# Three more two-level down products, deep weights stored in order of use, and later tokens' norms from row sums

## The chip, the cores and the metric

The kernel runs on one core of a Trainium2 chip. The time is device microseconds of one launch, from its first to its last instruction and a little around them. The kernel before was run four times: a median of 1454.92 us, from 1453.96 to 1455.33. One of these runs was profiled: 1455.33 us.

## What is computed

Four layers act in turn on x, 2048 tokens of 1024 features: A, B, A, B, each adding to x. A is linear attention with 32 heads, B is a gated MLP with an inner width of 3584:

```python
def _B_ref(x, W_gate, W_up, W_down):
    gate = jnp.einsum("bsd,df->bsf", x, W_gate)
    up = jnp.einsum("bsd,df->bsf", x, W_up)
    gate = gate * (lambda x, dt: x.astype(dt))(gate > 0, gate.dtype)
    h = gate * up
    return jnp.einsum("bsf,fd->bsd", h, W_down)

x = A_x
x = x + _A_ref(_layernorm(x, axis=-1), A_wqkv, A_wo)
x = x + _B_ref(_layernorm(x, axis=-1), B_W_gate, B_W_up, B_W_down)
x = x + _A_ref(_layernorm(x, axis=-1), A_wqkv, A_wo)
x = x + _B_ref(_layernorm(x, axis=-1), B_W_gate, B_W_up, B_W_down)
```

The layer norm has no weights: mean and variance over the 1024 features, 1e-5 under the root. Both B layers use the same three matrices, and so do both A layers.

## The kernel before

The tokens are 16 tiles of 128, and x stays in SBUF in float32 all the time. Layers are numbered 0 to 3, so B is layers 1 and 3. A B layer is worked in two chunks c of 8 tiles, written (1,0), (1,1), (3,0) and (3,1). A chunk is first 14 GLU units u, each for 256 of the 3584 columns (`glu`, L1129, with its matmuls on L1144), and then a down stage.

All large products use the Strassen–Winograd scheme: two operands cut in 2 x 2 blocks, seven products of blocks instead of eight, and sums of blocks before and after. In a down stage (`down_deep`, L1212) the left operand is h and its sums (four blocks of 512 tokens by 1792 features, "e" for two of the sums), the right one is W_down in blocks of 1792 by 512: the raw blocks 11, 21 and 22, and the sums T1 to T4, which are made once, on VectorE (`load_d`, `sums_d`, L1062 and L1076), and kept in DRAM in `td`. A plain product (`product`, L1247) is 4 token tiles by 14 matmuls of 512 columns. Results are added from PSUM into x by `onto` (L1263). A product of this stage can be *deep* (`deep`, L1291): the scheme once more inside it, with seven sub-products of two halves of 7 matmuls of 256 columns. Its left sums S1 to S4 are made on VectorE (`inner`, L1285, adds on L1283). Within a deep product three PSUM banks x, y and z are in use; ScalarE copies the first and fifth sub-products (L1315), VectorE makes the z sum out of the sixth and the copied fifth (L1325), and `put` adds each quarter of the result into x. T1's result goes into both token halves, so that its put (`put_both`, L1350) is two adds. The right sums of a deep product, four blocks of 896 by 256, are made once on VectorE (`load_dd`, `sums_dd`, L1011 and L1030) and stored in DRAM in `dd`.

Which products are deep is in `is_deep` (L974): T1, 22 and T4, in all chunks but (1,0), where an older function `down` (L1386, matmuls on L1418) does all seven plain. The deep blocks are made while the GLU of (1,1) runs, units 1 to 9. `td` is made earlier, the last two of its seven pairs of rows during the GLU of (1,0), one sum a unit in units 4 to 11. That GLU also makes the sums of the gate and up weights for later chunks (`make_gu`, L1050 to L1058, once per unit, ScalarE's queue stores them as tg and tu).

Weights come through a ring of slots in SBUF, filled ahead of use in the order in which they are used (`plan_B`, L955, on SP's DMA queue; plain entries on L968). A deep product takes four ring entries (`load_deep`, L993): an entry holds two blocks (the last one), a raw one read out of the matrix or `td` in rows of 256 elements (`load_raw`, L1003) and a made one out of `dd` (L1007). SP's queue works in order, and also holds the transposes of normed tiles (L399), the moves of x tiles to DRAM and back (`send_away`, `bring_back`, L258), and the stores of `td` and `dd` (L1078 and in `sums_dd`).

The normed tiles for a B layer are made in two ways. For tiles 0 to 7 the attention's last addition into x also sums each row (a scalar_tensor_tensor with an accumulator, L768, into `acc`), and ScalarE makes the sum of squares with an accumulating Square (`ln_norm_sums`, L204, L214 to L220). The later tiles 8 to 15 take statistics on VectorE (BN statistics, L162 to L167, then a shift on L196), in the down stage of (1,0) or (3,0) for the chunk that follows. The A layer that follows takes its first eight tiles' statistics in the same way. A normed tile is transposed by SP's DMA (L399), and then VectorE makes its sums for the GLU's scheme (`sums_x`, L1108, L1118 to L1121).

The program's order is written by hand: work for engines beside TensorE is put into a list `later` with a delay in ticks, a tick being called after each group of matmuls, so the delays set where in VectorE's and SP's in-order queues something lies. `behind` and `issue_after` hold an instruction back until after a given one in its queue. Where nothing holds it, an instruction may stand in its queue ahead of the place where it was written, as soon as its inputs are there: so the statistics for layer 2's first tiles, written in the down stage of (1,1), lie in that of (1,0).

Of the kernel before, what the change touches and what calls it, by code (L numbers as in the profile page):

```python
# [92 lines left out]
class _Net:  # L93
    def __init__(self, tc, ctx, x_d, wqkv_d, wo_d, wg_d, wu_d, wd_d, out_d):
# [34 lines left out]
        self.td = self.spill.tile([P, self.U, 4, NW], F16, name="td")  # L129
        self.tw = {n: self.spill.tile([P, 8, NW], F16, name=f"t{n}") for n in ("q0", "q1", "k0", "k1")}  # L130
        self.dd = {p: self.spill.tile([P, 4, self.U // 2, NW // 2], F16, name=f"dd{p}") for p in self.DEEP}
# [15 lines left out]
        self.x = [self.xall[:, t, :] for t in range(self.ST)]  # L147

        self.xb = [x[:, D // 2:D].bitcast(BF16) for x in self.x]
        self.xnT, self.xn, self.pk, self.slabs, self.xs, self.acc = {}, {}, {}, {}, {}, {}  # L150
# [29 lines left out]
    def ln_norm(self, layer, t):  # L180

        nc = self.nc
        if layer % 2 and t < self.NS:
            return self.ln_norm_sums(layer, t)
# [19 lines left out]
    def ln_norm_sums(self, layer, t):  # L204

        nc, src, acc = self.nc, self.x[t], self.acc[layer]
# [206 lines left out]
    def ln_later(self, layer, q, first, step, lag):  # L413
        for j in range(QT):
            self.ln_at(first + j * step, layer, q * QT + j, lag)
# [37 lines left out]
    def layer_A(self, l, last_ln):  # L453
# [298 lines left out]

        def out_unit(sc, j, n2):
            t = sc * QT + j
            ps = self.ps.tile([P, NW], F32, tag="a")
            for g in range(G):
                nc.tensor.matmul(ps, lhsT=pqT[sc][:, g, j * P:(j + 1) * P],  # L757
                                 rhs=T[g // 4][:, g % 4, n2 * NW:(n2 + 1) * NW],
                                 start=(g == 0), stop=(g == G - 1))
            cols = slice(n2 * NW, (n2 + 1) * NW)  # L760
            xs = self.x[t][:, cols]


            x0 = self.xb[t][:, cols] if l == 0 else xs
            if t < self.NS:
                if last_ln not in self.acc:
                    self.acc[last_ln] = self.const.tile([P, 2 * self.NS], F32, name=f"acc{last_ln}")
                self.last_x = nc.vector.scalar_tensor_tensor(  # L768
                    out=xs, in0=ps, scalar=0.0, in1=x0, op0=ALU.add, op1=ALU.add,
                    accum_out=self.acc[last_ln][:, 2 * t + n2:2 * t + n2 + 1])  # L770
            else:
                self.last_x = nc.vector.tensor_tensor(out=xs, in0=x0, in1=ps, op=ALU.add)


        def out_pairs(sc):
# [38 lines left out]
            def products():  # L814
# [4 lines left out]
                def onto(i, n, bank):  # L819
                    xs = half(self.x[sc * QT + i], n)  # L820
                    nc.vector.tensor_tensor(out=xs, in0=xs, in1=bank, op=ALU.add)

                for m, bank, start, n in ((1, X, True, None), (5, V, True, (2, 1)), (6, Y, False, (0, 1)),
                                          (2, X, False, (0, 0)), (7, Y, False, (2, 1)),
                                          (3, V, False, (0, 1)), (4, Y, False, (2, 0))):
                    for i in range(2):
# [6 lines left out]
                        else:  # L833
                            onto(n[0] + i, n[1], bank[i])
# [137 lines left out]
    DEEP = ("T1", "22", "T4")  # L972

    def is_deep(self, l, c, p):  # L974
        return (l, c) != (1, 0) and p in self.DEEP

    def order_d(self, l, c):
        if (l, c) == (1, 0):
            return "11", "21", "T1", "T2", "T3", "22", "T4"
        return "11", "21", "T1", "T2", "22", "T3", "T4"  # L980

    def src_d(self, p, us, cols=slice(0, NW)):
        if p[0] == "T":
            return self.td[:, us, self.T_AT[p], cols]
        n = (int(p[1]) - 1) * NW
        return self.wd_v[:, int(p[0]) - 1, us, n + cols.start:n + cols.stop]
# [6 lines left out]
    def load_deep(self, t, p, e):  # L993

        half, hn = self.U // 2, NW // 2
        v = self.deep_view(t)
        lo, hi = slice(0, half), slice(half, 2 * half)
        made = {0: (1, 0), 1: (0, 1), 2: (0, 2), 3: (0, 3)}[e]
        raw = {0: (0, lo, 0), 1: (1, hi, 0), 2: (1, hi, hn)}.get(e)

        def load_raw():
            src = self.src_d(p, raw[1], slice(raw[2], raw[2] + hn))
            self.nc.sync.dma_start(out=v[:, raw[0], :, :].bitcast(src.dtype), in_=src)  # L1003

        if raw and raw[0] == 0:
            load_raw()
        self.nc.sync.dma_start(out=v[:, made[0], :, :].bitcast(F16), in_=self.dd[p][:, made[1], :, :])  # L1007
        if raw and raw[0] == 1:
            load_raw()

    def load_dd(self, p):  # L1011

        half = self.U // 2
        self.deep_t = t = [self.slot(f"dd{p}{i}", [P, half, NW]) for i in range(2)]
        for out, us in ((t[0][:, :, :], slice(0, half)),
# [3 lines left out]
            self.nc.sync.dma_start(out=out.bitcast(src.dtype), in_=src)  # L1019

    def sums_dd(self, p, n):

        t = self.deep_t
        hn = NW // 2
        (b11, b12), (b21, b22) = ([x[:, :, i * hn:(i + 1) * hn] for i in range(2)] for x in t)
        f16 = lambda a: a.bitcast(F16)
        raw = f16 if p[0] == "T" else lambda a: a
        out, a, b = ((f16(b11), raw(b12), raw(b11)), (f16(b12), raw(b22), raw(b12)),
                     (f16(b22), raw(b22), f16(b11)), (f16(b21), raw(b21), f16(b22)))[n]
        self.nc.vector.tensor_tensor(out=out, in0=a, in1=b, op=ALU.subtract)  # L1030
        if n == 1:
            self.later.at(2, lambda: [self.nc.sync.dma_start(out=self.dd[p][:, m, :, :], in_=f16(b))
                                      for m, b in ((0, b11), (2, b12))])
        if n == 3:
            self.later.at(2, lambda: [self.nc.sync.dma_start(out=self.dd[p][:, m, :, :], in_=f16(b))
                                      for m, b in ((3, b21), (1, b22))])
# [31 lines left out]
    def sums_d(self, t, u, ops=range(4)):  # L1068

        T = t[:, :, :, :].bitcast(F16)  # L1070
        for n in ops:
# [5 lines left out]
            if n == 3:  # L1077
                self.later.at(2, lambda: self.nc.sync.dma_start(  # L1078
                    out=self.td[:, u:u + 2, :, :], in_=T))
# [43 lines left out]
    def ln_chunk(self, l, c, first, step, lag, after):  # L1123
        for j in range(QT):
            for h in range(2):
                self.ln_at(first + (2 * j + h) * step, l, (2 * c + h) * QT + j, lag, after)
            self.later.at(first + (2 * j + 1) * step + lag + (5 if l == 3 else 3), lambda j=j: self.sums_x(l, c, j))
# [84 lines left out]
    def down_deep(self, l, c, hT, final):  # L1212
# [27 lines left out]
        free = of_h(0)  # L1240
        S1, S2, S4, S3 = (cut(free[k], j) for k in range(2) for j in range(2))
# [43 lines left out]
        def inner(A):  # L1285
            (a11, a21), (a12, a22) = ([cut(A[k], j) for j in range(2)] for k in range(2))
            return (a11, a12, a21, a22), list(sums(((S1, a21, a22, ALU.add), (S2, S1, a11, ALU.subtract),
                                                    (S3, a11, a21, ALU.subtract),
                                                    (S4, a12, S2, ALU.subtract))))

        def deep(p, parts, put):  # L1291

            a11, a12, a21, a22 = parts
            B = {}

            def entry(e):
# [4 lines left out]
                lo, hi = lambda x: lambda i: x[:, i, :], lambda x: lambda i: x[:, (i + 1) % NK, :]  # L1301
                B.update(({1: lo(raw[:, 0]), 5: lo(made[:, 1])}, {6: lo(made[:, 0]), 2: hi(raw[:, 1])},
                          {7: lo(made[:, 0]), 3: hi(raw[:, 1])}, {4: lo(made[:, 0])})[e])

            def mm(m, A, bank, start=False):
                for j in range(2):
                    for i in range(NK):
                        nc.tensor.matmul(bank[:, j * H:(j + 1) * H],  # L1308
                                         lhsT=A[i // 2][:, i % 2, j * P:(j + 1) * P], rhs=B[m](i),
# [19 lines left out]
            put(1, 1, m5, False)  # L1329
# [3 lines left out]
            put(1, 1, y, True)  # L1333
            later.tick()
            mm(3, S4, z)
            put(0, 1, z, True)
            later.tick()
# [9 lines left out]

        both = self.xall[:, first:first + 2 * QT, :].rearrange("p (a j i) n -> p a j i n", a=2, i=2)
# [14 lines left out]

        product("11", raw(0), X, True, seed)
        parts, jobs = inner(of_e(e1))
        spread(jobs, 1, 3)
        product("21", raw(1), X, False, to(first, 0, X, True))
        for p, (_, b, _, _) in pairs:
            later.at(2 + p // 2, lambda b=b, p=p: v.tensor_tensor(out=b, in0=b, in1=part(e2, p),
                                                                 op=ALU.subtract))  # L1370
        deep("T1", parts, put_both)
        parts, jobs = inner(of_h(1))
        spread(jobs, 1, 2)
        product("T2", own(e2), Y, False, to(first, 1, Y, False))
        deep("22", parts, put_into(first, 1))
        parts, jobs = inner(of_h(3))
        spread(jobs, 1, 2)

        def third_done(j):
            to(second, 1, Y, True)(j)  # L1380
            to(second, 0, Y, False)(j)

        product("T3", raw(2), Y, False, third_done)
        deep("T4", parts, put_into(second, 0))

    def down(self, l, c, hT, final):  # L1386
        if (l, c) != (1, 0):
            return self.down_deep(l, c, hT, final)

        nc, later, ring, v = self.nc, self.later, self.ring, self.nc.vector  # L1390
        N = NW
        pairs = [(p, [x[:, b::4, :] for b in range(4)]) for p, x in enumerate(hT)]
        e1, e2 = ([self.slot(f"e{i}_{l}_{c}_{k}", dtype=F16) for k in range(2)] for i in (1, 2))
        part = lambda e, p: e[p // 4][:, (p % 4) * 2:(p % 4) * 2 + 2, :]
        with self.tc.issue_after(self.last_put.ins):
            for p, (a, _, g, d) in pairs:
                v.tensor_tensor(out=part(e1, p), in0=g, in1=d, op=ALU.add)
                v.tensor_tensor(out=part(e2, p), in0=part(e1, p), in1=a, op=ALU.subtract)
            for p, (a, _, g, d) in pairs:
                v.tensor_tensor(out=g, in0=a, in1=g, op=ALU.subtract)  # L1400
        raw = lambda b: lambda k: hT[k // 2][:, (k % 2) * 4 + b, :]
        own = lambda e: lambda k: e[k // 8][:, k % 8, :]
        X = [self.ps.tile([P, N], F32, tag="a", name=f"dx{j}") for j in range(QT)]
        Y = [self.ps3.tile([P, N], F32, tag="b", name=f"dy{j}") for j in range(2)]
        Y += [self.kvp.tile([P, N], F32, tag=f"kv{j}", name=f"dy{2 + j}") for j in range(2)]
        V = []
# [172 lines left out]
```

## Time and profile before

| what | value |
| --- | --- |
| median of four runs | 1454.92 us (1453.96 to 1455.33) |
| profiled execution | 1455.33 us, its span 1453.6 us |
| TensorE clock | 1.00 |
| TensorE busy | 1440.6 us, 99% of the span |
| VectorE busy | 952.4 us, 66% |
| ScalarE busy | 590.2 us, 41% |
| GLU of (1,0) | about 222 to 397 us, with the attention's last products of layer 0 among its first units |
| down stages | about 397 to 479 us (1,0), 651 to 740 (1,1), 1117 to 1200 (3,0), 1369 to the end (3,1) |

The profile gives, for each engine, the time in which it was busy. A window's row gives the busy time and number of instructions per engine in that stretch, the granted TensorE clock, and how busy the DMA engines were. The chain follows the work that ended last back to the start: each piece is an instruction (or several alike) that the next one waited for, or that stood before it on its engine. A group row gives instructions of one line and shape: their number, busy time, mean, and the idle time of the engine ahead of them with what ended it. A line number is that of the kernel before.

### The profile page before, as it was taken

The page shows a single profiled execution, that of the slowest core. Times are in us where ns is not written, and L with a number is a line of the kernel's source. Part 1 is how long each engine was busy: PE and PEld are TensorE (multiplying, and loading weights), DVE is VectorE, ACT ScalarE, POOL GpSimd, SP SyncE. Part 2 cuts the span into 40 slices and gives each one's busy share as a digit, 9 for nine tenths or more (in the row PEclk, how much of TensorE's full clock was granted, in tenths as well). Part 3 has the DMA queues.
Part 4 walks back from the last instruction along what each step waited for, and adds up shares of the span by engine and source line. Part 5 has one row for each costly group of instructions (what it writes and reads, how often), then busy time and mean ns, then how long its engine had stood idle before and what let it go on. Part 6 is the DMA issues. An engine that isn't in the chain of part 4 may idle for free.

```text
span 1453.6 us, 19816 instructions
## 1 busy us (share of the span) xinstructions
PE 1440.6 (99%) x7271; PEld 696.8 (48%) x7304; DVE 952.4 (66%) x1748; ACT 590.2 (41%) x1059; POOL 308.5 (21%) x221
## 2 busy tenths in 40 slices
PE   9999999999999999999999999999999999999998
PEld 4444444444444444445654444444444564444456
DVE  7978698666594555449688886766445864444574
ACT  7872574233340333332168626633333213333300
POOL 1453861011100011110031586410111011111001
PEclk9999999999999999999999999999999999999999
DMA  9840797664559999846983119975444799444473
GB/s 287 226 167 8 177 216 202 195 207 159 202 179 254 346 348 357 263 128 213 274 267 88 58 30 265 266 231 194 145 145 143 213 287 319 145 146 145 152 250 126
DMA packets 350801, 291.56 MB, mean 201 GB/s; under 512 B 107152, under 2 KB 317200, under 8 KB 348784
## 3 DMA queue, kind: packets, MB, share of 16 engines
q1 hardware_dynamic: 342656, 269.00, 63.0%
q10 hardware_dynamic: 6560, 17.24, 3.1%
q0 software_dynamic: 1488, 4.07, 0.8%
q8 instruction: 57, 0.93, 0.3%
q14 instruction: 40, 0.33, 0.1%
HBM read 221.32 MB, written 44.30 MB: 183 GB/s over the span
## 4 chain that ended last, share of the span: by engine, by line
PE 86%; DVE 7%; POOL 2%; DMA 1%; issue 1%; ACT 1%; SPq 1%; DVEq 0%; ACTq 0%; POOLq 0%
PE yg L1144 10%; PE yu L1144 10%; PE ps L479 10%; PE xu L1144 6%; PE xg L1144 6%; PE ps L757 4%; PE dy L1256 4%; PE zg L1144 3%; PE zu L1144 3%; PE dx L1256 3%; PE vu L1144 3%; PE vg L1144 3%; PE dy L1418 2%; PE mx L561 2%; PE dv L1418 2%; PE dx L1418 2%
## 5 line engine op out<-in xcount | busy, mean ns | idle before, releaser
L1144 PEld LDWEIGHTS <-w 128*128 128x128 f16 (+1 forms) x3136 | 306.6, 98 | 371.5 <-issue 2.2
L1197 POOL TENSOR_TENSOR h<-m5u,m5g 128x512 f16<-128x512 f32 x56 | 72.0, 1285 | 723.6 <-DVE m5u L1193 593.3
L479 PE MATMUL ps<-w,xnT 128*128 128x512 bf16 x768 | 170.0, 380 | 0.0
L1180 DVE TENSOR_TENSOR zg<-yg,m5g 128x512 f32<-128x512 f32 x56 | 39.1, 699 | 171.9 <-PE yg L1144 168.5
L479 PEld LDWEIGHTS <-xnT 128*128 128x128 bf16 x768 | 74.3, 98 | 89.8 <-issue 1.4
L1144 PE MATMUL yg<-s,w 128*128 128x512 f16 x448 | 115.0, 379 | 0.1
L1144 PE MATMUL xg<-xnT,w 128*128 128x512 f16 x448 | 115.0, 379 | 0.0
L1144 PE MATMUL yu<-s,w 128*128 128x512 f16 x448 | 115.0, 379 | 0.0
L1144 PE MATMUL xu<-xnT,w 128*128 128x512 f16 x448 | 115.0, 379 | 0.0
L1152 ACT ACTIVATE m5g<-m5g 128x512 f32<-128x512 f32 x56 | 35.2, 629 | 178.9 <-DVE m5g L1193 178.9
L422 ACT ACTIVATE e<-e,eps 128x512 f32<-128x512 f32 x128 | 91.0, 720 | 3.2
L709 POOL TENSOR_TENSOR kvc<-pq,kvc 128x1024 f32<-128x1024 bf16 x32 | 78.4, 2450 | 53.6 <-DVE den L714 33.3
L757 PE MATMUL ps<-T,pqT 128*128 128x512 bf16 x374 | 83.0, 380 | 0.5
L1308 PEld LDWEIGHTS <-h 128*128 128x128 f16 x756 | 74.0, 98 | 12.0 <-issue 2.0
L1256 PEld LDWEIGHTS <-h 128*128 128x128 f16 x504 | 49.4, 98 | 59.5 <-DMA w<-td 1.0
L1155 DVE TENSOR_TENSOR h<-yu,r 128x512 f16<-128x512 f32 x56 | 38.7, 691 | 55.1 <-PE yu L1144 55.1
L500 POOL TENSOR_TENSOR kvc<-kvc,slab 128x512 f32<-128x512 f32 x46 | 57.2, 1249 | 75.9 <-DVE slab L425 72.7
L1256 PE MATMUL dx<-w,h 128*128 128x512 bf16 x327 | 72.5, 379 | 0.5
L1161 ACT ACTIVATE m5g<-vg 128x512 f32<-128x512 f32 x56 | 33.4, 597 | 93.1 <-PE vg L1144 83.0
L1193 DVE TENSOR_TENSOR m5u<-yu,m5u 128x512 f32<-128x512 f32 x56 | 38.7, 691 | 49.5 <-PE yu L1144 49.4
L1152 ACT ACTIVATE r<-yg 128x512 f32<-128x512 f32 x56 | 33.4, 597 | 85.6 <-PE yg L1144 85.6
L421 ACT ACTIVATE e<-ps 128x512 f32<-128x512 f32 x92 | 54.2, 590 | 29.0 <-PE ps L479 29.0
(242 smaller groups left out, 2384.2 us busy)
## 6 DMA issues: line engine op xcount, KB each, us to landing
w<-in_B_W_gate_dram SPq DMA_DIRECT2D x56, 512.0 KB, 5.9
w<-in_B_W_up_dram SPq DMA_DIRECT2D x56, 512.0 KB, 5.6
w<-tg SPq DMA_DIRECT2D x42, 512.0 KB, 7.2
w<-tu SPq DMA_DIRECT2D x42, 512.0 KB, 6.7
w<-td SPq DMA_DIRECT2D x20, 896.0 KB, 5.0
w<-in_B_W_down_dram SPq DMA_DIRECT2D x18, 896.0 KB, 4.9
w<-ddT SPq DMA_DIRECT2D x24, 448.0 KB, 5.3
w<-in_A_wqkv_dram SPq DMA_DIRECT2D x8, 1024.0 KB, 7.3
```

Source lines behind the costliest of these rows:

```text
L421: nc.scalar.activation(out=e, in_=ps, func=ACT.Relu, scale=-1.0)
L422: nc.scalar.activation(out=e, in_=e, func=ACT.Exp, scale=-1.0, bias=self.eps6[:, 0:1])
L479: nc.tensor.matmul(by_row(ps), lhsT=self.xnT[l, l_q][:, kt, j * P:(j + 1) * P], rhs=w[:, kt, :].rearrange("p (b i d) -> p i b d", i=R, d=H ...
L500: nc.gpsimd.tensor_tensor(out=ksum[:, cols], in0=ksum[:, cols], in1=pk, op=ALU.add)
L709: nc.gpsimd.tensor_tensor(out=prod, in0=pq_of[sc, j], in1=zrow, op=ALU.mult)
L757: nc.tensor.matmul(ps, lhsT=pqT[sc][:, g, j * P:(j + 1) * P], rhs=T[g // 4][:, g % 4, n2 * NW:(n2 + 1) * NW], start=(g == 0), stop=(g == G ...
L1144: nc.tensor.matmul(ps, lhsT=W[w][m][:, k, :], rhs=A[m][:, k, :], start=start and k == 0, stop=k == 3, skip_group_check=True)
L1152: self.last_relu = nc.scalar.activation(out=out, in_=ps, func=ACT.Relu)
L1197: nc.gpsimd.tensor_tensor(out=h[:, 3, :], in0=V["u"], in1=V["g"], op=ALU.mult)
L1256: nc.tensor.matmul(banks[j], lhsT=A(k)[:, j * P:(j + 1) * P], rhs=w[:, i, :], start=start and k == 0, stop=k == self.U - 1, skip_group_che ...
L1308: nc.tensor.matmul(bank[:, j * H:(j + 1) * H], lhsT=A[i // 2][:, i % 2, j * P:(j + 1) * P], rhs=B[m](i), start=start and i == 0 and j == 0 ...
L1418: nc.tensor.matmul(banks[j], lhsT=A(k)[:, j * P:(j + 1) * P], rhs=w[:, i, :], start=start and k == 0, stop=k == self.U - 1, skip_group_che ...
```

## The change

Five things are changed together.

1. Three more down products are deep: T1 and 22 in (1,0), and 21 in (3,1). In (3,1) the order is now 11, T2, T1, T3, 21, 22, T4. The function `down_deep` becomes the only `down`, with a case for each list.
2. `dd` holds all seven right blocks of a deep product, raw ones too, in order of use, so a ring entry is one contiguous DMA. `td` is laid out product by product instead of row pair by row pair; a pair is stored in four DMAs instead of one, and each deep sum in one of its own.
3. Where the deep blocks are made: those of 22 and T1 in the GLU of (1,0), T4's in the GLU of (1,1), those of 21 in the GLU of (3,0). The last two row pairs of `td` are loaded at unit 3 of (1,0) and their eight sums made in units 4 to 6.
4. All tiles of a B layer's norm use row sums (`add_up`), the later tiles too. The statistics of layer 2's first tiles are held until after unit 6 of the GLU of (1,1).
5. In T1 the put of the fifth sub-product moves behind that of the third (`early`), and closes that quarter instead of opening it.

```diff
-    DEEP = ("T1", "22", "T4")
+    DEEP = ("T1", "22", "T4", "21")
     def is_deep(self, l, c, p):
-        return (l, c) != (1, 0) and p in self.DEEP
+        return p in {(1, 0): ("T1", "22"), (3, 1): self.DEEP}.get((l, c), self.DEEP[:3])
     def order_d(self, l, c):
-        if (l, c) == (1, 0):
-            return "11", "21", "T1", "T2", "T3", "22", "T4"
+        if (l, c) == (3, 1):
+            return "11", "T2", "T1", "T3", "21", "22", "T4"
         return "11", "21", "T1", "T2", "22", "T3", "T4"
...
     def load_deep(self, t, p, e):
+        n = min(2, 7 - 2 * e)
+        self.nc.sync.dma_start(out=self.deep_view(t)[:, 0:n, :, :].bitcast(F16),
+                               in_=self.dd[p][:, 2 * e:2 * e + n, :, :])
...
+    def make_dd(self, p, at):
+        self.later.at(at, lambda: self.load_dd(p))
+        for n in range(4):
+            self.later.at(at + 18 + 4 * n, lambda n=n: self.behind(self.last_put, lambda n: self.sums_dd(p, n), (n,)))
...
             if n == 3:
-                self.later.at(2, lambda: self.nc.sync.dma_start(
-                    out=self.td[:, u:u + 2, :, :], in_=T))
+                self.later.at(2, lambda: [self.nc.sync.dma_start(
+                    out=self.td[:, m, u:u + 2, :], in_=T[:, :, m, :]) for m in range(4)])
...
     def ln_norm(self, layer, t):
-        if layer % 2 and t < self.NS:
+        if layer % 2:
             return self.ln_norm_sums(layer, t)
...
+        def add_up(t, n2, xs, ps, x0):
+            return nc.vector.scalar_tensor_tensor(
+                out=xs, in0=ps, scalar=0.0, in1=x0, op0=ALU.add, op1=ALU.add,
+                accum_out=self.acc[:, 2 * t + n2:2 * t + n2 + 1])
...
             mm(2, a12, x)
             put(0, 0, x, True)
-            put(1, 1, m5, False)
+            early = p != "T1"
+            if early:
+                put(1, 1, m5, False)
             later.tick()
             entry(2)
             mm(7, S3, y)
-            put(1, 1, y, True)
+            put(1, 1, y, early)
             later.tick()
             mm(3, S4, z)
             put(0, 1, z, True)
+            if not early:
+                put(1, 1, m5, True)
...
-                    if u in (3, 7):
-                        d = self.U - 4 + u // 4 * 2
-                        wd[d] = self.load_d(d)
-                    if 3 < u < 12:
-                        self.later.at(4, lambda d=self.U - 4 + (u - 4) // 4 * 2, n=(u - 4) % 4: behind(
-                            self.last_put, lambda: self.sums_d(wd[d], d, (n,))))
+                    if u == 3:
+                        for d in (self.U - 4, self.U - 2):
+                            wd[d] = self.load_d(d)
+                        self.make_dd("22", 18)
+                    if u in (4, 5, 6):
+                        for i, n in enumerate(range(3 * (u - 4), min(3 * (u - 3), 8))):
+                            self.later.at(2 + 4 * i, lambda d=self.U - 4 + n // 4 * 2, n=n % 4: behind(
+                                self.last_put, lambda: self.sums_d(wd[d], d, (n,))))
+                    if u == 7:
+                        self.make_dd("T1", 1)
...
-                if not final and c == 1:
-                    if u in (1, 4, 7):
-                        self.later.at(1, lambda p=self.DEEP[u // 3]: self.load_dd(p))
-                    if u in (2, 3, 5, 6, 8, 9):
-                        for n in range(2):
-                            self.later.at(2 + 5 * n, lambda p=self.DEEP[(u - 2) // 3], n=2 * ((u - 2) % 3) + n: behind(
-                                self.last_put, lambda: self.sums_dd(p, n)))
+                if (l, c, u) in ((1, 1, 6), (3, 0, 4)):
+                    self.make_dd("T4" if l == 1 else "21", 1)
...
+                if c == 1 and u == 6:
+                    held = self.last_put.ins
...
-                self.ln_later(l + 1, 0, 25, 3, 4)
-                self.ln_later(l + 1, 1, 37, 3, 4)
+                self.ln_later(l + 1, 0, 25, 3, 4, held)
+                self.ln_later(l + 1, 1, 37, 3, 4, held)
```

The case of `down` for (3,1), where three deep products follow one another:

```diff
+        if self.is_deep(l, c, "21"):
+            product("11", raw(0), X, True, eleven_done)
+            parts, jobs = inner(of_e(e1), room(0))
+            spread(jobs, 1, 3)
+            product("T2", own(e2), Y, False, to(first, 1, Y, False))
+            for p, (_, b, _, _) in pairs:
+                later.at(2 + p // 2, lambda b=b, p=p: sub(part(e2, p), b, part(e2, p)))
+            deep("T1", parts, put_both)
+            parts, jobs = inner(of_h(1), room(0))
+            spread(jobs, 1, 3)
+            product("T3", raw(2), Y, False, third_done)
+            parts2, jobs = inner(of_e(e2), room(2))
+            spread(jobs, 1, 4)
+            deep("21", parts, put_into(first, 0))
+            parts, jobs = inner(of_h(3), room(0))
+            spread(jobs, 1, 4)
+            deep("22", parts2, put_into(first, 1))
+            deep("T4", parts, put_into(second, 0))
+            return
```

## The prediction

> **What bounds the kernel now.** I read the page's busy table and the chain's shares first, then the chain piece by piece, the stages by window, VectorE's groups and the DMA issues.
>
> ```profile
> PE 1440.6 (99%) x7271; PEld 696.8 (48%) x7304; DVE 952.4 (66%) x1748; ACT 590.2 (41%) x1059; POOL 308.5 (21%) x221
> PE 86%; DVE 7%; POOL 2%; DMA 1%; issue 1%; ACT 1%; SPq 1%; DVEq 0%; ACTq 0%; POOLq 0%
> ```
>
> TensorE is busy for 99% of the span and carries 86% of the chain: only fewer matmul columns, or one of its few pauses, can move the end. The chain by pieces (start, length, what, how many) shows two prices and the pauses:
>
> ```profile
> 420.84 12.09 PE dv L1418 x56
> 695.16 5.53 DMA w<-td
> 1161.43 4.49 DMA xnT<-xnb
> 1172.13 1.69 PE dy L1308 x14
> 1393.04 1.53 PE dxT L1308 x14
> 1401.46 1.21 DVE x L1269 x2
> 1404.39 11.87 PE dy L1256 x55
> 1416.26 1.53 PE dx L1308 x14
> 1427.18 11.87 PE dy L1256 x55
> ```
>
> A plain down product is 56 matmuls of 512 columns in 12.09 us (215.8 ns each). A deep one is seven sub-products of 14 matmuls of 256 columns in 1.53 us (109.2 ns each), 10.70 us. In chunk (3,1) the plain T3 and the deep 22 together run from 1404.39 to 1427.18, 22.79 us or 12.09 + 10.70: no pause in either. Deep T1, from 1393.04 to 1404.39, takes 11.35 us where 22 takes 10.92 by the same marks; it waits for VectorE's adds into x (the piece at 1401.46).
>
> The windows (length, then busy PE, PEld, DVE, ACT, POOL, clock, DMA share, GB/s) of a GLU unit of chunk (1,0), and of the down stages of (1,0), (3,0) and (3,1):
>
> ```profile
> 301.00:313.00 12.00, 12.00 (x58) 5.41 (x56) 7.92 (x15) 4.58 (x9) 1.27 (x1) 1.00 0.60 177
> 397.00:493.00 96.00, 95.79 (x442) 43.49 (x446) 64.64 (x135) 21.88 (x44) 1.27 (x1) 1.00 0.80 242
> 1117.00:1210.00 93.00, 91.11 (x565) 55.46 (x567) 66.36 (x141) 20.36 (x33) 10.27 (x16) 1.00 0.92 263
> 1369.00:1454.00 85.00, 80.31 (x515) 50.40 (x516) 57.17 (x117) 5.87 (x10) 9.43 (x15) 1.00 0.61 193
> ```
>
> VectorE has 4 us free in a GLU unit of 12. Its groups (busy and mean, idle before) price what is moved, and the DMA issues (KB each, us to landing) the loads:
>
> ```profile
> L162 DVE BATCH_NORM_STATS2 stats<-x 128x6 f32<-128x512 f32 x64 | 40.9, 668 | 0.2
> L1030 DVE TENSOR_TENSOR ddT<-ddT 128x1792 f16<-128x1792 f16 x4 | 4.3, 1087 | 0.1
> ...
> w<-td SPq DMA_DIRECT2D x20, 896.0 KB, 5.0
> ...
> w<-td SPq DMA_DIRECT2D x18, 448.0 KB, 6.0
> ```
>
> **The sum** goes against the profiled execution, 1455.33 us (span 1453.6 and 1.7 outside it). The median of the four runs shown, 1454.92, is 0.41 lower; 0.41 comes off at the end.
>
> *Products: -4.17.* Three times, 56 matmuls of 512 columns become 98 of 256 (T1 and 22 in (1,0), 21 in (3,1)): 3 x (12.09 - 10.70), on an engine with no slack to hide it. The changed instruction list holds 168 fewer of 512 and 294 more of 256. If deep T1 of before were the pattern, 11.35 less the 0.22 that the marks shift, it would be 3 x 0.96 = 2.9. I take 4.17, since T1's excess has its own cause, the next term.
>
> *T1's puts: -0.9.* A put of T1 is two adds of 0.6 us each, one for each token half. The put of the fifth sub-product stood ahead of the z sum and the y put that free the next banks; now it goes behind the third sub-product. T1's excess was 0.43 in (3,1) and (3,0), and 0.65 in (1,1), 1.5 in all. Bounds 0 and 1.5. One double put still lies between the seventh sub-product and the fourth's bank: 1.2 us in a sub-product of 1.53, so by the order some 0.15 to 0.25 stays each time. T1 in (1,0) then has the same: +0.15.
>
> *Ring loads: -1.9.* A deep ring entry was two loads of 448 KB, in part in rows of half a block; now it is one of 896 KB, and that size lands no later (5.0 us against 6.0). Two pauses of before hang on SP: at 1172.13 TensorE lost 1.6 us since the deep 22's z sum stood on VectorE behind the x sums, and these behind transposes whose issue held SP for 3.48 and 2.26 us, right behind five of these loads; at 700.74 it lost 0.9 us on a load issued at 695.16, behind two such transposes. Bounds: 0 and 2.5. Half the loads and longer rows leave less in front of a transpose, so I take three quarters. Next late are the waits at layer 2's start (0.3 and 1.2 us near 755), which stay.
>
> *Weight sums in GLU (1,0): +1.7.* All eight sums of the last two row pairs now fall in units 4 to 6 (before: one a unit), and 22's four block sums in one unit. VectorE in the fullest unit: 7.92, less one pair sum (0.69), plus three of them (2.06), plus four of L1030 (4.35), is 13.6 in 12.09. Along the order of VectorE's and TensorE's instructions, with the groups' durations, the bank that the next matmul needs (zg, zu, zg) comes late by 0.4, 0.6 and 0.4, and 0.2 once more later. Bounds 0 and 3. T1's block sums fall where there are no pair sums: 7.92 - 0.69 + 4.35 = 11.6, covered; without that cover 0.5 more.
>
> *Slots and SP there: +0.5.* Block and pair tiles take buffers from the weights' pool, and two up loads now wait for a matmul that stands 3.6 us ahead of the weights' sums (in TensorE's steps). Up loads land in 5.1 there: VectorE is 1.5 us late, of which the next unit's slack takes about 1. Bounds 0 and, if they land in 7.2 as the tg loads do, 4. The stores of pair sums (7 to 28) and of block sums (12 to 28) also go ahead of weight loads on SP; they wait for sums that VectorE has done by then, so nothing more.
> [...]
>
> *GLU (1,1): +0.8.* 32 of L162 leave down (1,0): 16 go (row sums do their work), 16 for layer 2 move here, beside T4's four block sums. A unit: seven adds of 0.69, 4.35, and nine of 0.67, 15.2 us in 12.09. Stats can slip between, so by the order there are late banks of 0.4 and 0.2, and two more of 0.1. Bounds 0 and 3.1.
>
> *Norms by row sums: 0.* 16 squares of 1.14 us come to ScalarE, busy 21.88 of 96 us in down (1,0); the 32 added accumulator reads of 0.08 come where VectorE idles. In (1,0) the deep 22's z sum now stands behind x sums as in (3,0): bounds 0 and 1.6. I take 0, as by the order those x sums are done some 2 us before the z sum is due; the first rival prices the rest.
>
> *Three deep in a row (21, 22, T4): 0.* 896 KB in 3.06 us is 300 GB/s, against 193 in that window and 357 in the page's best slice. At 200 the shortfall over 32 us is 3.2 MB, and five ring entries hold 4.6. Bounds 0 and the third rival.
>
> Sum: -4.17 - 0.9 + 0.15 - 1.9 + 1.7 + 0.5 + 0.8 = -3.8. 1455.33 - 3.8 - 0.41 = **1451.1 us**.
>
> **Rivals.** *The DMA pauses stay, and come to (1,0) too*: +1.9 + 1.6, 1454.6. For it: a norm by row sums has 1.33 us more on ScalarE (square and read) before its transpose. Against: the loads in front are halved.
>
> *Slower: the loads of GLU (1,0) land late.* In GLU (1,1) of before the block loads themselves took 9.2 us (896 KB) and 10.8 (768 KB). If the weight loads beside them land in 8.5 instead of 5.1, each of the two loses 3.4 us more, and a third, issued behind a store that waits for a block load, about 1.5: 1451.1 + 8.3 = 1459.4. It decides from 6.7 us (landing at 7.9 or so). Against: the window's DMA share of 0.60.
>
> *The triple is starved*: at 250 GB/s with an empty ring, 32 x 50/250 = 6.4 us, 1457.5. Against: a plain T3 stands before it to fill the ring.
>
> *VectorE's excess is absorbed*: without the +1.7, +0.5 and +0.8, 1448.1. For it: 4 us free in the units around.
>
> That it doesn't do what it says is excluded by the instruction list.
>
> **How the numbers follow.** Likeliest 0.60 (own range 1449.4 to 1452.8), absorbed 0.18, pauses stay 0.10, late loads 0.07, starved 0.05. A change of 0.2% (2.9 us) is about what a measurement of this kernel can tell: below 1452.0 is faster, up to 1457.8 the same. Faster: 0.48 of the first and 0.18, 0.66; same: 0.12 + 0.10 + 0.02, 0.24; slower: 0.07 + 0.03, 0.10. The range leaves out late loads, starved, and the lower end of absorbed: 1447.3 to 1455.3.
>
> **What would show it.** Right: PE busy about 4 us lower; T1 and 22 of (1,0) and 21 of (3,1) at 10.7 to 10.9 us; T1 at 11.1 or less; pauses of about half a us near 297, 300 and 311. Wrong: pauses above 1 us there with weights' sums or a DMA as releaser, z sums that wait for transposes in (1,0), 21 waiting for w.

## The result and the profile after

| | median | range, runs |
| --- | --- | --- |
| before | 1454.67 us | 1453.56 to 1459.16, 53 |
| after | 1453.55 us | 1450.54 to 1455.95, 33 |

The ratio is 0.9989, with a 95% interval of 0.9984 to 0.9994: 1.6 us faster by the ratio, 1.1 by the two medians, a change below the 0.2% that the prediction took as its bound for "the same". 1451.1 us was predicted, with a range of 1447.3 to 1455.3, 0.66 for faster and 0.24 for the same: the time lies in the range, it came out as the same, and under half of the gain came. The profiled execution of the change took 1452.19 us, 1.4 below its median; that of before took 1455.33, 0.7 above its own. The 3.1 us between the two profiles are thus more than the change is worth.

The page of the changed kernel, its busy times and the chain's shares by engine:

```profile
PE 1438.0 (99%) x7400; PEld 709.6 (49%) x7430; DVE 959.4 (66%) x1799; ACT 613.4 (42%) x1113; POOL 309.8 (21%) x221
PE 93%; DVE 4%; ACT 1%; issue 1%; DMA 0%; DVEq 0%; ACTq 0%
```

TensorE's busy time fell by only 2.6 us although 4.17 us of columns went, and VectorE's share of the chain fell from 7% to 4%. The chain by pieces shows that the new deep products run as hoped. First T1, T2 and 22 in (1,0):

```profile
421.06 1.53 PE dxT L1305 x14
...
430.45 1.66 PE dyT L1305 x14
432.10 11.87 PE dy L1253 x55
443.97 1.53 PE dx L1305 x14
...
453.15 1.53 PE dy L1305 x14
454.68 24.17 PE dy L1253 x112
```

T1 takes 11.04 us (421.06 to 432.10; 11.35 for that of before in (3,1)) and 22 takes 10.71. In (3,1), 21, 22 and T4 follow one another from 1414.51 to 1446.62, 32.1 us or three times 10.70, with no pause. The place that counts is in (3,0), in the chain and then in windows of 1 us (length, busy PE, PEld, DVE, ACT, POOL, granted clock, DMA share, GB/s):

```profile
1160.37 1.53 PE dx L1305 x14
1161.90 1.53 PE dz L1305 x14
1163.42 1.53 PE dy L1305 x14
1164.95 1.54 PE dx L1305 x14
...
1168.41 0.62 DVE dz L1322
...
1169.08 3.15 PE dy L1305 x14
1172.22 1.68 PE dz L1305 x14
```

```profile
1168.00:1169.00 1.00, 0.00 (x0) 0.00 (x0) 1.00 (x4) 0.48 (x2) 0.00 (x0) 0.99 0.73 244
1169.00:1170.00 1.00, 0.92 (x5) 0.67 (x5) 1.00 (x4) 0.94 (x1) 0.00 (x0) 0.50 1.02 401
1170.00:1171.00 1.00, 1.00 (x7) 0.69 (x6) 0.15 (x1) 1.00 (x8) 0.56 (x1) 0.50 1.07 282
1171.00:1172.00 1.00, 1.00 (x6) 0.71 (x5) 0.80 (x2) 1.00 (x3) 0.15 (x1) 0.50 1.12 240
1172.00:1173.00 1.00, 1.00 (x10) 0.82 (x8) 0.78 (x3) 1.00 (x2) 0.00 (x0) 0.80 0.19 58
1173.00:1174.00 1.00, 1.00 (x12) 0.90 (x10) 1.00 (x4) 0.54 (x1) 0.72 (x1) 1.00 0.00 0
```

The deep 22 stops after its fourth sub-product at 1166.3, until VectorE has made the z sum: a pause of 2.76 us where before there were 1.62 (a pause is counted here from the time at which the next matmul would have started to the time at which it did). The two places side by side, of the changed kernel and then of the one before; in brackets is the idle time of the engine and what ended it:

```profile
1169.08 3.15 PE L1305 MATMUL dy<-w,h 128*128 128x256 f16 x14 [2.60 <-DVE dz L1322]
```

```profile
1172.13 1.69 PE L1308 MATMUL dy<-w,h 128*128 128x256 f16 x14 [1.46 <-DVE dz L1325]
```

In the changed kernel the granted clock then stands at 0.50 for 3.4 us. The next sub-product takes 3.15 us instead of 1.53: about 15 matmuls start 213 ns apart, not 109 (15 x 0.103 = 1.55 us). This place costs 2.76 + 1.55 = 4.3 us, 2.7 more than before. TensorE is "busy" in the slow matmuls, so only a part of this shows as idle time.

What held VectorE is in its waits between 1150 and 1170 us, of the changed kernel and then, between 1150 and 1173, of the one before (waited for: us in total, times, longest):

```profile
DVE s L1114 <- DMA xnT<-xnb: 3.0, 1, 3.0
```

```profile
DVE s L1118 <- DMA xnT<-xnb: 1.8, 1, 1.8
```

The first of the x sums for the next chunk waits for a transposed tile, with the work for 22 behind it in the queue. After T2's start (1148.50 after, 1152.69 before) that tile came 14.4 us later, where before it had come 13.3 us later: the 1.1 us by which the pause grew. It was not issued later: SP issued its transpose 8.4 us after T2's start (at 1156.86), before 8.7 us after it (at 1161.43). But it landed 6.0 us after its issue, where before it had taken 4.5. An earlier transpose held SP for 4.59 us, from 1150.20, behind three loads of 896 KB; the three that stand ahead of the awaited one took 7.3 us of SP together, and 7.2 before, so that hold is not the difference.

### The profile page after: what moved, and what is told of

Read it like the earlier page. It is cut to its first block, busy times and chain, and to the rows that moved or that the text cites. A ratio compares the mean times of both kernels' runs of the same rounds, so it can differ in the third digit from the quotient of the medians.

```text
span 1450.4 us, 20236 instructions
## 1 busy us (share of the span) xinstructions
PE 1438.0 (99%) x7400; PEld 709.6 (49%) x7430; DVE 959.4 (66%) x1799; ACT 613.4 (42%) x1113; POOL 309.8 (21%) x221
## 4 chain that ended last, share of the span: by engine, by line
PE 93%; DVE 4%; ACT 1%; issue 1%; DMA 0%; DVEq 0%; ACTq 0%
PE yu L1140 10%; PE yg L1140 10%; PE ps L480 10%; PE dy L1253 7%; PE xg L1140 6%; PE xu L1140 6%; PE dx L1253 6%; PE ps L763 4%; PE zu L1140 3%; PE zg L1140 3%; PE vg L1140 3%; PE vu L1140 3%; PE my L562 3%; PE dyT L1305 2%; PE mv L562 2%; PE mx L562 2%
## 5 line engine op out<-in xcount | busy, mean ns | idle before, releaser
L1253 PEld LDWEIGHTS <-h 128*128 128x128 f16 x672 | 65.7, 98 | 78.3
L1305 PEld LDWEIGHTS <-h 128*128 128x128 f16 x966 | 95.3, 99 | 15.9 <-issue 2.8
L1253 PE MATMUL dx<-w,h 128*128 128x512 bf16 x381 | 84.7, 379 | 0.6
```

Of the source, the lines that this page charges most:

```text
L1253: nc.tensor.matmul(banks[j], lhsT=A(k)[:, j * P:(j + 1) * P], rhs=w[:, i, :], start=start and k == 0, stop=k == self.U - 1, skip_group_che ...
L1305: nc.tensor.matmul(bank[:, j * H:(j + 1) * H], lhsT=A[i // 2][:, i % 2, j * P:(j + 1) * P], rhs=B[m][:, i, :], start=start and i == 0 and ...
```

## The experiments

"The fix" below is the move of all x sums in the third experiment.

**The same x sums, moved in the kernel before.** The sums of the first two tile groups in (3,0) are held behind 22's z sum:

```diff
+            self.z_sum = v.tensor_tensor(out=z, in0=y, in1=m5, op=ALU.add)
...
+            if l == 3 and j < 2:
+                self.later.at(36 + 3 * j, lambda j=j: self.behind(self.z_sum, lambda k: self.sums_x(l, c, k), (j,)))
```

> The kernel before, with the same move of the x sums in (3,0) alone. Theory: its pause of 1.6 us before 22's sixth result is used goes, nothing else moves: 1454.7 - 1.6 = 1453.1. If the order of x sums isn't what holds the z sum: no change, 1454.7.

Measured: 1452.15 us against 1453.70 on the same chip, ratio 0.9990 (0.9981 to 0.9999). The pause of 1.62 us is gone and no other pause takes its place, so the order of x sums did hold the z sum. The other two long waits of the profile of before, at 700 and at 882 us, are also shorter in this one: 0 instead of 0.87 and 0.32 instead of 1.07, though the kernel is the same there.

**The same in the changed kernel.**

> The changed kernel, but in (3,0) the x sums of the first two tile groups for the next chunk are issued on VectorE only after the z sum of the deep 22, and not before it. Theory (the gain was eaten at one place: the x sums wait there for a transpose, 22's z sum stands behind them, TensorE pauses 2.8 us, and after it runs 16 matmuls at half clock, 1.7 us more): pause and slow matmuls both go, granted clock 1.000 in the runs, about 4.4 us less than the profiled run of the change, 1447.8, a median near 1448.5. Rival (the z sum is late through VectorE's load at that place, whatever stands in front): pause stays above 1.5 us, 1452 to 1454. Rival (the lower clock is the chip's and not the pause's): pause goes, clock still below 1.000 in half of the runs, 1450 to 1452.

Measured: 1449.75 us against 1453.70, ratio 0.9976 (0.9966 to 0.9987); the profiled execution took 1450.09. Two of the eight runs took 1453 us, one of them at a clock of 0.998. In 22 there is no pause and no slow matmul. But T4 now has one of 2.22 us. Its chain:

```profile
1171.49 10.89 DMA xnT<-xnb
1182.41 0.42 DVE s L1114
...
1190.73 0.57 DVE dzT L1325
1191.35 1.69 PE dyT L1308 x14
```

The transpose of the third tile group, 10.89 us from issue to landing, now holds up VectorE's adds for T3, and with them T4's z sum. The theory on 22 stood, its number did not: part of the wait had moved, as the next case shows. The matmuls behind the pause start 109 ns apart, so this pause of 2.22 us did not lower the clock.

**All four groups of x sums held**, the last two behind T4's z sum:

```diff
+            if l == 3:
+                self.later.at((36, 39, 50, 51)[j], lambda j=j: self.behind(self.z_sum, lambda k: self.sums_x(l, c, k), (j,)))
```

> The changed kernel with all four groups of x sums of (3,0) held: the first two behind the z sum of 22, the other two behind the z sum of T4. With only the first two held, TensorE paused 2.2 us in T4 instead (VectorE waited 8.3 us for a transpose that held SP for 4.3 us). Theory: no pause of over 0.2 us is left in that down stage, clock 1.000: 1450.1 - 2.2 = 1447.9 for the profiled run, a median of 1447.5 to 1448.5. Rival (the wait moves again, into the first GLU unit of (3,1), which needs the sums): 1449 to 1450.

Measured: 1448.24 us (1447.91 to 1449.70) against 1453.69, ratio 0.9964 (0.9951 to 0.9976): better than both kernels, by 5.4 us against before and by some 3.8 against the change. In the kernel before, the move of its one wait brought 1.6. Its chain in (3,0):

```profile
1160.76 1.53 PE dx L1308 x14
...
1169.93 1.53 PE dy L1308 x14
1171.45 12.09 PE dy L1256 x56
1183.54 1.53 PE dxT L1308 x14
...
1192.71 1.53 PE dyT L1308 x14
1194.24 0.86 PE vg L1143 x4
```

22, T3, T4 and the next GLU follow without a pause.

**Are the row sums why the transposes are late?** Layer 3's later tokens go back to BN statistics, in the changed kernel:

```diff
-        if layer % 2:
+        if layer == 1 or layer == 3 and t < self.NS:
             return self.ln_norm_sums(layer, t)
```

> The changed kernel, with the later tokens' norms of layer 3 by BN statistics on VectorE as before (layer 1 keeps row sums). Rival for the longer pause in (3,0): row sums put a square of 1.1 us on ScalarE before each transpose. If so: pause back to about 1.6 us, no slow matmuls, 1449.5. Theory (the transposes are late through SP, where one of them takes 4.6 us behind three loads of 896 KB): pause stays 2 to 3 us and the time within 1 us of the change, 1453.5.

Measured: 1452.95 us against 1453.70, ratio 0.9994 (0.9985 to 1.0003). The pause in the profiled execution is 2.94 us, with 15 slow matmuls behind it. The rival on ScalarE falls. The theory's own reason, a transpose that is late through SP, is not shown by that: the awaited transpose landed 5.7 us after its issue here too.

**Is the size of a load the reason?** Each deep ring entry is loaded in two halves:

```diff
-        self.nc.sync.dma_start(out=self.deep_view(t)[:, 0:n, :, :].bitcast(F16),
-                               in_=self.dd[p][:, 2 * e:2 * e + n, :, :])
+        for m in range(n):
+            self.nc.sync.dma_start(out=self.deep_view(t)[:, m, :, :].bitcast(F16),
+                                   in_=self.dd[p][:, 2 * e + m, :, :])
```

> The changed kernel, with each deep ring entry loaded block by block: two loads of 448 KB, contiguous rows of 3.5 KB, in place of one of 896 KB. If the size of a load in front of a transpose on SP is what holds it: the transpose in (3,0) is issued earlier, pause 1.5 us or less, about 1449.5. If it's the bytes in the queues: same pause and time as the change, 1453.5. [...]

Measured: 1453.16 us against 1453.70, ratio 0.9996 (0.9987 to 1.0005), a pause of 3.36 us with 13 slow matmuls. One transpose held SP for 5.11 us there. The size of one load is not the reason. The awaited transpose landed 4.4 to 4.5 us after its issue in the four profiles with the old down stage in (3,0), and 5.6 to 6.4 in nine of the ten with the new one. The tenth, the one with T1 and 22 of (1,0) plain, has 4.5 with the same order in (3,0). So the down stage's own loads alone do not decide it, and what does was not shown. In this run there is also a pause of 0.32 us before 22's sixth result is used in (1,0), and two in the GLU of (1,0), of 0.68 and 0.64 us.

**The change once more**, and two kernels that were to lengthen the pause of the kernel before by one or two copies on VectorE in front of 22's z sum in (3,0):

```diff
+            for _ in range(2 if (l, c, p) == (3, 0, "22") else 0):
+                m6 = self.temp(name="dm5")
+                v.tensor_copy(out=m6, in_=m5)
+                m5 = m6
```

> The changed kernel itself once more, beside the next two. Theory (the pause in (3,0) is near a length at which the clock falls, and its length changes from run to run): a pause of 2 to 3.5 us before the sixth result of 22 is used; if above some 2.5 us, 13 to 16 matmuls at half clock behind it; times from 1450.5 to 1456, the higher ones with a clock below 1.000.

> The kernel before, with one copy on VectorE (0.6 to 0.7 us) put between the fifth result and the z sum of 22 in (3,0), so the pause there grows from 1.6 to about 2.3 us. Theory (a pause of 2.2 us left the clock alone, one of 2.8 halved it): no slow matmuls, 0.7 us more. Rival (any longer pause costs clock): slow matmuls behind it.

> As the one with one copy, but two copies one after the other: pause about 3.0 us. Theory: 13 to 16 matmuls at half the clock behind it, 1.4 to 1.7 us more on top of the 1.4 us of pause, 3 us in all. Rival (the lower clock in the change has nothing to do with the pause): 1.4 us more, all matmuls at 109 ns.

Measured: the change took 1452.46 us (1450.97 to 1454.40) against 1454.09, ratio 0.9990 (0.9980 to 0.9999), with a pause of 2.99 us and 12 slow matmuls in its profile. The kernels with copies took 1455.38 and 1455.25 us in one run each. The copies failed in their purpose: each takes 0.42 us, one of the sums that had stood in front of the z sum now stands behind it, and the pauses came out at 1.36 and 1.55 us, with no slow matmul. They say nothing on longer pauses.

**A pause made by VectorE alone**, ten such copies on top of the fix:

> As the one with all x sums of (3,0) held, with ten copies one after the other on VectorE between the fifth result of 22 and its z sum in (3,0): a pause that no transfer has a part in, of about 3.3 us (10 x 0.45 us less what slack there is). (One and two copies in the kernel before took only 0.4 us each and left its pause at 1.4 and 1.5 us.) Theory (a pause of TensorE of some 2.5 us and more costs clock after it): 12 to 16 matmuls at 213 ns behind it, 1448.2 + 3.3 + 1.5 = 1453.0. Rival (the half clock belongs to what the DMA engines do there): all matmuls at 109 ns, 1451.5.

Measured: 1449.56 us against 1453.90, ratio 0.9966 (0.9954 to 0.9978). Again no long pause came of it: 17 matmuls of T3 stand ahead of the sub-product that waits, and pauses of 0.12 and 0.55 us are left. So a long pause without busy DMA engines beside it was not obtained, and whether the clock falls there too stays open.

**The parts of the change, undone on top of the fix.** T1 and 22 of (1,0) plain again:

```diff
-        return p in {(1, 0): ("T1", "22"), (3, 1): self.DEEP}.get((l, c), self.DEEP[:3])
+        return p in {(1, 0): (), (3, 1): self.DEEP}.get((l, c), self.DEEP[:3])
...
+            product("T1", own(e1), V, True, to(second, 1, V, False))
+            product("T2", own(e2), Y, False, to(first, 1, Y, False))
...
+            product("22", raw(1), V, False, first_done)
```

> As the one with all x sums held, but T1 and 22 of (1,0) plain again (their deep blocks are still made at the same places, for the later chunks). Theory: two deep products are worth 2 x 1.39 us less 0.13 of pause in T1: 2.65 us slower than with them, near 1450.5. Rival (their gain is lost to waits in (1,0)): within 1 us.

Measured: 1451.94 us, 3.7 above the fix (ratio to before 0.9988, 0.9979 to 0.9997). In the two profiles the stretch from the start of T1 to the end of that down stage is 60.43 us (421.57 to 482.00) against 57.78 (421.43 to 479.21), 2.65 more, as expected. What else the two profiles differ by (4.1 us in all) is not the products': pauses of 0.40 at 330 us, 0.31 at 701 and 0.09, and 0.9 more behind TensorE's end, less a start that was 0.3 earlier.

21 plain again, in the old order:

```diff
-        return p in {(1, 0): ("T1", "22"), (3, 1): self.DEEP}.get((l, c), self.DEEP[:3])
+        return p in {(1, 0): ("T1", "22")}.get((l, c), self.DEEP[:3])
```

> As the one with all x sums held, but without the deep 21 in (3,1), in the order of before and without making its blocks in the GLU of (3,0). Theory: 1.4 us slower, near 1449.3. Rival (three deep products in a row are starved of weights): no slower.

Measured: 1450.92 us, 2.7 above the fix (ratio to before 0.9979, 0.9970 to 0.9988). In the profiles, TensorE ends 2.0 us later, at 1444.62 against 1442.63: 1.4 for the product, and 0.6 from elsewhere, pauses of 0.8 in the GLU and the down stage of (1,0) less a start that was 0.25 earlier. Another 0.6 lies behind TensorE's end. One of these pauses, at 330 us, has this chain:

```profile
319.26 8.18 DMA w<-in_B_W_up_dram
...
327.46 0.69 DVE w L1049
...
330.20 1.02 PE xu L1141 x4
```

This is an up load that landed after 8.2 us, with VectorE's sums of weights behind it and 0.45 us of pause on TensorE.

T1's put back at its old place, in all four chunks:

```diff
-            early = p != "T1"
+            early = True
```

> As the one with all x sums held, but T1's put of the fifth sub-product stands ahead of the third again, in all four chunks. Theory: pauses of 0.3 to 0.7 us in each T1 come back, 0.3 to 0.45 more in (1,0), (3,0) and (3,1) each and 0.3 in (1,1): 1.2 to 1.6 us slower, near 1449.3. Rival (the order of that put doesn't matter): no difference.

Measured: 1450.14 us, 1.9 above the fix (ratio to before 0.9974, 0.9964 to 0.9984). T1's pauses are 0.41 in (1,0), 0.33 and 0.32 in (1,1), 0.44 in (3,0) and 0.66 in (3,1), against 0.13, 0.31, 0.13 and 0.13: 1.45 us. A weight load's pause of 0.30 at 330 us comes on top.

The three parts come to 8.3 us by their medians, more than the 5.4 by which the fix is faster than the kernel before: the profile of the fix has no pause at 330 us, each of these three has one, and two of them end later behind TensorE. By lengths within the profiles the parts are 2.65, 1.4 and 1.45.

## Why the prediction was right in its range and wrong in its sum

The terms against the two profiled executions (pauses of TensorE above 0.08 us, start to start):

| term | predicted | measured |
| --- | --- | --- |
| products | -4.17 | -4.17 by their lengths (3 x 1.39) |
| T1's puts, with T1 of (1,0) | -0.75 | -0.83 |
| load pause at 700 us | -0.65 | -0.87, but see below |
| 22's pause in (3,0) | -1.2 | +1.14, and 1.55 by the clock |
| weight sums in GLU (1,0) | +1.7 | +0.47 |
| slots there | +0.5 | 0 here; 0.3 to 0.7 for the load in other profiles |
| GLU (1,1) | +0.8 | +0.42 |
| wait for the output weights at 882 us | 0 | -0.76, but see below |
| z sum of 22 in (1,0) | 0 | 0 |
| three deep in a row | 0 | 0 |

**Products, right.** T1 and 22 in (1,0) and 21 in (3,1) cost what their matmuls cost; the triple wasn't starved.

**Two waits of the profile of before belong to that execution.** The pauses at 700 us (0.87) and 882 us (1.07) stand in the one profile that was read. The three other profiles of kernels that are the same as before up to the down stage of (3,0) have no pause at 700 us and 0.32, 0.37 and 0.44 us at 882. In the one with the x sums moved, T2 runs through where before it waited for the load:

```profile
686.20 11.87 PE dy L1259 x55
```

So the -0.87 and most of the -0.76 are one execution against another; that the change took them away is not shown, and a profile of the change with T1 and 22 of (1,0) plain has a pause of 0.31 us at 701 us.

**T1's puts, right**, the residue too: 0.13 us stays in three of the four chunks, and 0.31 in (1,1).

**The ring loads: this is the step that failed.** "Half the loads and longer rows leave less in front of a transpose, so I take three quarters" was false in (3,0), and at 700 us it could not be told. In (3,0), with half the loads for the same bytes (three of 896 KB; before six of 448 KB, where the prediction counts five), the awaited transpose was issued 0.4 us earlier after T2's start than before, but it took 1.5 us longer to land, so that the tile came 1.1 us later. The term counted on the issue and left out the landing. The bounds were a gain of 0 to 2.5 us; with the two places together it was a loss of 1.8 (1.14 + 1.55 - 0.87). The rival "the DMA pauses stay" was the nearer to what happened, though its reason and its second place were not: row sums on ScalarE do not make the pause, and (1,0) has none in this profile. What neither had is the clock: a pause of TensorE was priced by its length alone. Why the landing took longer stays open.

**Weight sums in GLU (1,0) and (1,1): the mechanism right, the sizes 2 to 4 times too large.** The rival "VectorE's excess is absorbed" was the nearer: of 3.0 us for these and the slots, 0.9 came. The windows of the fullest units after:

```profile
289.00:301.00 12.00, 12.00 (x57) 5.41 (x56) 11.27 (x19) 4.55 (x9) 1.99 (x1) 1.00 1.00 315
301.00:313.00 12.00, 11.70 (x55) 5.23 (x54) 9.74 (x18) 4.26 (x8) 1.27 (x1) 1.00 1.02 331
```

VectorE was busy for 11.27 of 12 us, not for 13.6 of 12.09. The sum added durations (0.69, 1.09), but an instruction starts before the one in front has ended: the adds of 0.69 us start 0.60 apart where nothing is waited for. And the extra work didn't all meet in one unit. One pause of 0.47 us is left, at 307 us.

**Slots: right in kind.** In the profiled execution the up loads came in time; in five of the other profiles of the changed kernel one or two did not, by 0.30 to 0.68 us. The slower rival, by which the loads of the GLU of (1,0) land in 8.5 us, is seen in its cause (8.2 us for the load shown) and not in its price of 3.4 us for each: TensorE paused 0.45 us behind that load.

**The sign.** Errors of both kinds partly met, and that the time lies in the range owes something to this luck: VectorE's and the slots' terms were 2.1 us too dear, the pause in (3,0) was 3.9 too cheap, and the wait at 882 us gave 0.8 that nobody had forecast. In the profiled executions that leaves 0.7 us between forecast change (-3.8) and measured one (-3.1). The median lies worse, and the clock has a part in it: of the 34 runs with a clock on record (one more than in the table), the 8 with a mean clock of 1.000 took 1450.5 to 1452.2 us, the 9 with 0.999 took 1451.3 to 1454.7, the 17 with 0.998 took 1452.2 to 1456.0.

The cleanest comparison leaves the wait in (3,0) out on both sides: 1452.15 us for the kernel before with its x sums moved, 1448.24 for the change with all of them moved, each beside a kernel before at 1453.7. That is -3.9. The prediction's terms without its two ring-load terms come to -1.9, and -4.0 once the 2.1 us that were too dear are taken off. The two agree more closely than the runs can vouch for: the intervals of the two ratios are 1.3 and 1.8 us to either side.

**The split stores, no term of their own.** In the GLU of (1,0) a store of 256 KB landed in 4.7 us (median of 8), one of 1 MB before in 6.6 (median of 2). The DMA share in the window from 301 to 313 us rose from 0.60 to 1.02 (row above), but that window also has the new block loads in it, so the stores' part isn't known.

## What to carry to other kernels

Before a change is costed, look at what stands in front of a result that the bounding engine needs, in the same in-order queue, and waits for a DMA: work that is not urgent (here sums for the next stage) belongs behind the urgent result. Moving all of it made no new pause here, moving half of it did; the move brought 1.6 us in the kernel before and 3.8 in the changed one, more than the change itself. Price a long pause of TensorE by its length and by the slow matmuls behind it: here pauses of 2.76 us and more had 12 to 15 of them, 1.55 us in the changed kernel. Look for a pause in a second profile of the same code before it is priced as a gain. Fill a queue by the distance between starts of its instructions, not by their durations.

## What the runs showed of the hardware

In four profiles the granted clock fell to 0.50 behind a pause of TensorE: pauses of 2.76, 2.94, 2.99 and 3.36 us (the change, layer 3 with BN statistics, the change once more, the loads in halves) were followed by 15, 15, 12 and 13 matmuls of 256 columns about 213 ns apart. Pauses of 2.22, 1.62, 1.55, 1.36 and 1.19 us were followed by none. The slow stretch lasted 3.41 us each time (1168.98 to 1172.40, 1170.21 to 1173.62, 1168.60 to 1172.01 and 1170.90 to 1174.32, in the order of the four pauses). It began 2.2 to 3.6 us after the pause did, in one profile only when TensorE had run again for 0.7 us. All four are at the same place with busy DMA engines, and a pause without them could not be made. None of these pauses is between 2.22 and 2.76 us, so what length is safe was not shown, nor what sets the length of the slow stretch.

The shortest issue of a DMA transpose on SP's queue took 1.23 us in the profiles of before and after. The longest of those behind the deep 22's loads in (3,0) held SP for 3.48 us before and for 4.59 with the loads of 896 KB, and for 5.11 with these in two pieces.
